# Linear attention into a snake MLP on one core: another way to turn the first chunk's q and k, and a new order table

## Chip, core and metric

The kernel runs on one core of a Trainium2 chip. The metric is the device time of one execution in microseconds (us), lower is better. Engine names: TensorE (PE) multiplies matrices and turns tiles by a matmul with the identity; VectorE (DVE) and ScalarE (ACT) do elementwise work; GpSimd (POOL) does elementwise work and issues software loads that cast fp32 to bf16 on the way; SyncE (SP) issues hardware loads and stores, which ACT can issue too. Results of TensorE lie in eight PSUM banks, everything else on chip in SBUF.

## What is computed

Inputs: q, k, v of 4 batches x 8 heads x 768 tokens x 64 features, a decay `lam` per head, and the weights of an MLP (512 to 2048 to 512 features). The reference works in blocks of 64 tokens; the kernel uses 128, which gives the same sum.

```python
Dmask = where(rel >= 0, lam ** rel, 0.0)             # rel = token i - token j, within a block
for b in range(nb):
    intra = (q_b @ k_b.T * Dmask) @ v_b
    inter = (q_b * lam ** (pos + 1)) @ kv_state
    out[block b] = intra + inter
    kv_state = lam ** block * kv_state + (k_b * lam ** (block - 1 - pos)).T @ v_b
x = out, all heads side by side                       # 3072 x 512
h = x @ w_in
g = h + sin(alpha * h) ** 2 / (alpha + 1e-09)
result = g @ w_out                                    # 3072 x 512
```

## The kernel before

There are six chunks of 128 tokens (t = 0 to 5), each with all four batches. A chunk's attention gives `xt[t]` (512 features x 512 columns of 4 batches x 128 tokens); the MLP of the same group g = t follows, in 16 slices f of 128 hidden features. Attention of later chunks is laid between the MLP work of earlier groups.

Nothing schedules by itself: every engine runs its instructions in the order in which the program issues them, and after a hand-written start that order is the table `ORDER`, one word per step. `h g.f:bank` is a hidden slice (four matmuls of 512 columns, L325), `s` its sine on ACT (L330), `q`, `Q` and `P` its square on ACT (L336), on DVE as a multiply (L338) or on DVE in a three-operand form (L340), `t` the finish on DVE that writes a slice of `gall` and frees the bank (L345). `u g.m.part` is four matmuls of the output projection with one quarter of w_out (L352), `o` its copy and store. For attention: `r`, `R`, `n`, `v` load a later chunk's k and q in the "raw" form (32 partitions, rows of four tokens) and its k and v in the natural form (token per partition), `I` and `W` load a quarter of w_in and of w_out, all through POOL. `z` scales raw q by the decay on POOL (L264), `k` and `j` turn raw k and q with DVE in pairs of bf16 values moved as fp32 (L240), `F` is the scores (L249), `m` the masks (L255), `d` scales natural k on POOL (L260), `K` makes the state's increment (L274), `S` adds it up, `B` and `C` cast it on ACT and POOL, `O` is the carried and the inner outputs (L295, L304), `x` their way into `xt`.

The mask table `C0` (L226) holds lam^-(j+1) for j not after i; the other factor lam^(i+1) is put on q ahead of the scores.

The first chunk goes another way, because there is no carried state and everything waits for it. q of batches 0 and 1 comes through SP as fp32 in rows of 64 values (L150) and is scaled by DVE (L419); q of batches 2 and 3 comes through POOL (a load of 256 KB) and is left unscaled, its factor being put on the output by the table `Etab` (L223, L416). k and v come through POOL. TensorE turns both k and q, 16 transposes each (L387), ACT or DVE copies them out of PSUM (L390, L392), `scores0` multiplies 64-row halves (L398) and masks (L403), `outs0` multiplies with v (L410) and moves the result into `xt[0]` (L414, L416). Matmuls on a constant tile (`spin`, L192) keep TensorE busy meanwhile. Then the table's words begin. The last output tile is done in two halves by `project_halves` (L367).

POOL's software loads take turns on eight semaphores, so that the ninth load waits at its issue until the first has landed.

Of the kernel before, what the change touches and what calls it, by code (L numbers as in the profile page):

```python
# [33 lines left out]
z4.0 F3.1:3054 o1.3 t2.12 u2.0.0:6 m3.1.0 h2.13:1 m3.1.1 z4.1 u2.0.1 m3.1.2 s2.13 m3.1.3 h2.14:2 j4.0 O3:7305
s2.14 Q2.13 q2.14 t2.13 t2.14 u2.0.2 x3.0 d4.0 j4.1 x3.1 h2.15:4 x3.2 x3.3 F4.0:1273 s2.15 d4.1 h3.0:0 m4.0.0
q2.15 m4.0.1 h3.1:5 s3.0 t2.15 h3.2:1 q3.0 m4.0.2 s3.1 t3.0 K4:24 s3.2 m4.0.3 u2.0.3 q3.1 S4.0 q3.2 h3.3:7 t3.1
o2.0 B4.0 u2.1.0:0 t3.2 r5 s3.3 S4.1 F4.1:3265 q3.3 u2.1.1 m4.1.0 B4.1 m4.1.1 h3.4:1 R5 m4.1.2 u2.1.2 m4.1.3
s3.4 t3.3 h3.5:4 q3.4 t3.4 v5 O4:3265 s3.5 k5.0 q3.5 u2.1.3 x4.0 t3.5 x4.1 k5.1 h3.6:7 x4.2 x4.3 h3.7:1 z5.0
o2.1 s3.6 u2.2.0:3 s3.7 h3.8:4 q3.6 z5.1 j5.0 q3.7 u2.2.1 s3.8 t3.6 F5.0:2650 q3.8 t3.7 u2.2.2 t3.8 h3.9:7
m5.0.0 m5.0.1 u2.2.3 s3.9 m5.0.2 h3.10:1 q3.9 m5.0.3 o2.2 u2.3.0:4 t3.9 s3.10 j5.1 h3.11:2 q3.10 t3.10 u2.3.1  # L40
s3.11 q3.11 F5.1:6503 u2.3.2 t3.11 m5.1.0 h3.12:7 m5.1.1 u2.3.3 m5.1.2 s3.12 m5.1.3 h3.13:1 q3.12 o2.3 t3.12
O5:2650 s3.13 q3.13 t3.13 u3.0.0:3 h3.14:4 u3.0.1 s3.14 h3.15:7 q3.14 t3.14 u3.0.2 x5.0 x5.1 h4.0:1 x5.2 x5.3
h4.1:4 s3.15 h4.2:2 s4.0 q3.15 h4.3:6 q4.0 t3.15 h4.4:5 s4.1 t4.0 s4.2 u3.0.3 q4.1 q4.2 h4.5:0 t4.1 o3.0 t4.2
u3.1.0:7 s4.3 s4.4 h4.6:1 q4.3 u3.1.1 q4.4 t4.3 s4.5 h4.7:4 t4.4 s4.6 u3.1.2 q4.5 q4.6 t4.5 h4.8:3 s4.7 t4.6
u3.1.3 q4.7 s4.8 t4.7 h4.9:2 o3.1 q4.8 u3.2.0:6 s4.9 t4.8 h4.10:5 q4.9 u3.2.1 t4.9 s4.10 u4.0.0:0 q4.10 t4.10
u3.2.2 h4.11:1 u3.2.3 s4.11 u4.0.1 q4.11 o3.2 t4.11 h4.12:4 u4.0.2 s4.12 h4.13:7 q4.12 t4.12 h4.14:3 s4.13
u4.1.0:2 q4.13 s4.14 t4.13 h4.15:5 q4.14 u4.1.1 t4.14 s4.15 h5.0:6 q4.15 t4.15 u4.1.2 s5.0 u4.0.3 q5.0 u4.1.3
o4.0 h5.1:1 o4.1 u3.3.0:4 s5.1 u4.2.0:7 q5.1 u3.3.1 h5.2:3 u3.3.2 s5.2 u4.2.1 q5.2 u3.3.3 h5.3:5 t5.0 o3.3
u4.2.2 t5.1 s5.3 t5.2 h5.4:0 q5.3 t5.3 u4.2.3 s5.4 h5.5:2 q5.4 o4.2 t5.4 u4.3.0:4 s5.5 h5.6:6 q5.5 t5.5 u4.3.1
s5.6 h5.7:1 q5.6 t5.6 u4.3.2 s5.7 h5.8:3 q5.7 t5.7 u4.3.3 s5.8 h5.9:5 q5.8 o4.3 t5.8 h5.10:7 s5.9 u5.0.0:0 q5.9  # L50
s5.10 t5.9 h5.11:2 q5.10 u5.0.1 t5.10 s5.11 h5.12:6 q5.11 t5.11 h5.13:1 s5.12 u5.0.2 q5.12 s5.13 t5.12 h5.14:4
q5.13 u5.1.0:3 t5.13 s5.14 h5.15:5 q5.14 t5.14 u5.1.1 s5.15 u5.2.0:7 q5.15 t5.15 u5.1.2 u5.0.3 u5.1.3 o5.0
u5.2.1 o5.1 u5.2.2 u5.2.3 o5.2
# [4 lines left out]
def kernel(  # L58
# [11 lines left out]
    nc = tc.nc  # L70
# [77 lines left out]
    raw_q0 = gbp.tile([P, 2, H, D], FP32, name="raw_q0", tag="gall")  # L148
    for b in range(2):
        nc.sync.dma_start(out=raw_q0[:, b], in_=q[b, :, 0:T, :].rearrange("h p e -> p h e"))  # L150
    alpha_fp = consts.tile([NFC, P], FP32, name="alpha_fp")
    A.dma_start(out=alpha_fp[:], in_=moe_alpha.rearrange("(f p) -> f p", p=P))
    new_nat(0, "k")
    new_nat(0, "v")
    nat["q", 0] = rawp.tile([P, B, H, D], BF16, name="raw_q")
    load_nat(0, "k", 0)
    load_nat(0, "k", 1)
    pcol = consts.tile([P, 3], FP32, name="pcol")

    def token_column(n, base, step):  # L160
        G.iota(out=pcol[:, n:n + 1], pattern=[[0, 1]], base=base, channel_multiplier=step,
               allow_small_or_imprecise_dtypes=True)
# [48 lines left out]
    def power(tab, n):  # L211
        A.activation(out=tab[:], in_=lnlam[:], func=ACTF.Exp, scale=pcol[:, n:n + 1])
# [312 lines left out]
```

## Time and profile before

| what | us |
|---|---|
| median of 3 runs (210.4 to 211.32) | 211.24 |
| the profiled execution | 212.47 |
| its span, first to last instruction | 210.8 |
| TensorE busy in it | 197.1 |
| ACT busy | 148.1 |
| DVE busy | 135.7 |
| POOL busy | 100.8 |

Busy times overlap. A matmul is counted from its start to the end of its result, so a mean of 0.38 us per matmul of 512 columns is its latency; they start 0.216 us apart when nothing is waited for. A line of a group reads: code line, engine, operation, what is written from what, shapes, count, busy time and mean in ns, idle time of the engine before it and what ended that. A line of the chain reads: start, length, what. "DMA w_out" there is the time from a load's issue to its landing. Landing times of single loads come from the semaphore events of the trace, of which a load has 16, one for each DMA engine. About one matmul record in thirty is missing.

### The profile page before, as it was taken

How to read it: one execution, taken by the hardware profiler on the slowest of the kernel's cores; microseconds unless marked ns; L12 is line 12 of the kernel's file. 1: busy time of each engine (PE TensorE's matmuls, PEld its weight loads, DVE VectorE, ACT ScalarE, POOL GpSimd, SP SyncE). 2: the span in 40 equal slices, each digit the busy share in tenths (PEclk: the TensorE clock that was granted, in tenths of full speed). 3: DMA queues.
4: the chain of work that ended last, by engine and by line, in shares of the span. 5: the costliest groups of instructions: out<-in, count | busy, mean ns of one | idle time of the engine just before them, and what ended most of it. 6: DMA issues, size and time to landing. Idle time of an engine off the chain costs nothing.

```text
span 210.8 us, 4860 instructions
## 1 busy us (share of the span) xinstructions
PE 197.1 (94%) x1992; PEld 97.7 (46%) x2021; DVE 135.7 (64%) x201; ACT 148.1 (70%) x258; POOL 100.8 (48%) x116
## 2 busy tenths in 40 slices
PE   7958988699999999999999999999999999999993
PEld 3543433345444455444554544544444444444452
DVE  3996789571989998699999967715551503445400
ACT  4684959005998945998697968569975855889531
POOL 7999749758999994997694600000000000000000
PEclk9999999799999999999999999999999999999999
DMA  8999999999999699499969911100111020100022
GB/s 124 156 151 182 205 193 162 165 197 166 229 165 166 77 145 183 48 142 157 157 75 166 116 53 50 51 2 0 53 50 50 0 100 35 70 16 33 0 105 98
DMA packets 68920, 22.61 MB, mean 107 GB/s; under 512 B 50834, under 2 KB 65954, under 8 KB 68898
## 3 DMA queue, kind: packets, MB, share of 16 engines
q0 software_dynamic: 63184, 15.47, 79.6%
q1 hardware_dynamic: 5680, 6.82, 9.4%
q8 instruction: 16, 0.26, 0.5%
q14 instruction: 6, 0.05, 0.1%
q10 hardware_dynamic: 34, 0.01, 0.0%
HBM read 31.47 MB, written 6.29 MB: 179 GB/s over the span
## 4 chain that ended last, share of the span: by engine, by line
PE 74%; DMA 11%; DVE 5%; POOL 4%; ACT 2%; issue 2%; DVEq 0%; ACTq 0%; POOLq 0%
PE ops L352 35%; PE hps L325 29%; DMA w_in<-in_moe_w_in_dram 4%; DMA w_out<-in_moe_w_out_dram 4%; DMA nat_k<-in_k_dram 3%; PE F_ps L249 3%; PE O_ps L304 2%; DVE gall L345 2%; POOL nat_k L260 2%; DVE STm L255 2%; PE hps L367 2%; PE O_ps L295 2%; POOL w_in L141 1%; DVE S L283 1%; PE T_ps L387 1%
## 5 line engine op out<-in xcount | busy, mean ns | idle before, releaser
L345 DVE SCALAR_TENSOR_TENSOR gall<-s,r_sb,hps 128x512 bf16<-128x512 bf16 x96 | 69.3, 742 | 46.9 <-ACT s L336 36.8
L325 PE MATMUL hps<-xt,w_in 128*128 128x512 bf16 x372 | 90.9, 379 | 2.0 <-issue 0.7
L352 PE MATMUL ops<-w_out,gall 128*128 128x512 bf16 x352 | 88.1, 382 | 4.0 <-DMA w_out<-in_moe_w_out_dram 2.4
L330 ACT ACTIVATE s_sb<-hps,alpha_sb 128x512 bf16<-128x512 f32 x96 | 64.2, 692 | 27.7 <-PE hps L325 27.5
L325 PEld LDWEIGHTS <-w_in 128*128 128x128 bf16 x384 | 36.7, 98 | 46.0 <-issue 2.2
L352 PEld LDWEIGHTS <-gall 128*128 128x128 bf16 x368 | 35.1, 98 | 44.8 <-issue 3.7
L336 ACT ACTIVATE s<-s_sb 128x512 bf16<-128x512 bf16 x86 | 52.9, 638 | 1.6
L255 DVE TENSOR_TENSOR STm<-F_ps,C 128x512 bf16<-128x512 f32 x40 | 25.0, 683 | 4.2 <-PE F_ps L249 4.1
L260 POOL TENSOR_TENSOR nat_k<-nat_k,R 128x1024 bf16<-128x1024 bf16 x10 | 19.1, 1933 | 4.5 <-DMA nat_k<-in_k_dram 4.4
L264 POOL TENSOR_TENSOR raw_q<-raw_q,Rraw 128x1024 bf16<-128x1024 bf16 x10 | 18.9, 1919 | 4.0 <-DMA raw_q<-in_q_dram 4.0
L314 ACT CAST xt<-O_ps 128x512 bf16<-128x512 f32 x20 | 10.3, 600 | 14.9 <-PE O_ps L304 14.5
L358 ACT COPY o_sb<-ops 128x512 f32<-128x512 f32 x23 | 13.5, 592 | 8.0 <-PE ops L352 6.2
L240 DVE STREAM_TRANSPOSE turned_q<-raw_q 128x512 f32<-128x512 f32 x10 | 11.1, 1114 | 5.6 <-POOL raw_q L264 5.6
L131 POOL DMA_DIRECT2D nat_v<-in_v_dram x12 | 14.0, 1170 | 0.2 <-issue 0.2
L124 POOL DMA_DIRECT2D raw_k<-in_k_dram x20 | 11.7, 598 | 3.9 <-DMA w_out<-in_moe_w_out_dram 2.9
L124 POOL DMA_DIRECT2D raw_q<-in_q_dram x20 | 11.6, 588 | 4.0 <-DMA w_in<-in_moe_w_in_dram 2.6
L131 POOL DMA_DIRECT2D nat_k<-in_k_dram x10 | 11.8, 1190 | 0.8 <-POOLq L509 0.8
L240 DVE STREAM_TRANSPOSE turned_k<-raw_k 128x512 f32<-128x512 f32 x10 | 11.0, 1117 | 0.1
L338 DVE TENSOR_TENSOR s<-s_sb 128x512 bf16<-128x512 bf16 x9 | 5.9, 657 | 2.4 <-ACT s_sb L330 2.4
L249 PEld LDWEIGHTS <-turned_k 32*128 32x128 bf16 x320 | 5.0, 96 | 4.6 <-issue 3.8
L249 PE MATMUL F_ps<-turned_q,turned_k 32*128 32x128 bf16 x320 | 6.8, 224 | 0.0
L192 PE MATMUL spare<-fill 128*128 128x512 bf16 x11 | 5.0, 607 | 1.5 <-DVE one L174 1.5
(68 smaller groups left out, 97.9 us busy)
## 6 DMA issues: line engine op xcount, KB each, us to landing
out_dram<-o_sb SPq DMA_DIRECT2D x23, 256.0 KB, 2.6
nat_v<-in_v_dram POOLq DMA_DIRECT2D x12, 256.0 KB, 7.4
nat_k<-in_k_dram POOLq DMA_DIRECT2D x10, 256.0 KB, 7.6
raw_k<-in_k_dram POOLq DMA_DIRECT2D x20, 128.0 KB, 7.3
raw_q<-in_q_dram POOLq DMA_DIRECT2D x20, 128.0 KB, 5.6
w_out<-in_moe_w_out_dram POOLq DMA_DIRECT2D x4, 512.0 KB, 9.6
w_in<-in_moe_w_in_dram POOLq DMA_DIRECT2D x6, 256.0 KB, 8.1
raw_q<-in_q_dram SPq DMA_DIRECT2D x2, 256.0 KB, 3.6
```

The costliest lines, as they stand in the source:

```text
L124: (eng or G).dma_start(out=dst[quad[a], bs].rearrange("t b n r d -> t (b n) (r d)"), in_=src[t, a])
L131: G.dma_start(out=nat[nm, t][:, bs].rearrange("p b h e -> p (b h) e"), in_=SRC[nm][bs, :, t * T:(t + 1) * T, :].rearrange("b h p e -> p (b ...
L240: V.transpose(out=dst.rearrange("p (x t r) -> p x r t", r=R, t=32), in_=src.rearrange("p (x r d) -> p x r d", r=R, d=32))
L249: nc.tensor.matmul(out=F[a][:, u, n, :], lhsT=KQ["k", t][quad[a], 2 * pr + u, n, :, e], rhs=KQ["q", t][quad[a], 2 * pr + u, n, :, e], star ...
L255: V.tensor_tensor(out=st[t, pr][:, a], in0=att["F", pr][a], in1=C0[:, a].unsqueeze(1).broadcast_to([P, 2, NQ, T]), op=ALU.mult)
L260: G.tensor_tensor(out=kd, in0=kd, in1=R128[:].unsqueeze(1).unsqueeze(3).broadcast_to([P, 2, H, D]), op=ALU.mult)
L264: G.tensor_tensor(out=qs, in0=qs, in1=Rraw[:].rearrange("p n r -> p (n r)").unsqueeze(1).unsqueeze(3).broadcast_to([P, 2, NQ * R, D]), op= ...
L325: nc.tensor.matmul(out=hps[g, f][:], lhsT=w_in_sb[f // 4][:, c, (f % 4) * P:(f % 4 + 1) * P], rhs=xt[g][:, c, :], start=(c == 0), stop=(c ...
L330: A.activation(out=s_of[g, f][:], in_=hps[g, f][:], func=ACTF.Sin, scale=alpha_sb[:, f:f + 1])
L336: A.activation(out=s2_of[g, f][:], in_=s_sb[:], func=ACTF.Square)
L345: V.scalar_tensor_tensor(out=gall[g][:, f, :], in0=s2_of.pop((g, f))[:], scalar=r_sb[:, f:f + 1], in1=hps.pop((g, f))[:], op0=ALU.mult, op ...
L352: nc.tensor.matmul(out=ops[g, m][:], lhsT=gall[g][:, f, m * P:(m + 1) * P], rhs=w_out_sb[part][:, f % 4, :], start=(f == 0), stop=(f == NF ...
```

## The change

In the first chunk, all of q comes as fp32 in the raw form (rows of 1 KB) in eight hardware loads, six by SP and two by ACT. DVE casts it to bf16 and turns it as in later chunks. k is loaded by POOL per batch for the first two batches, and turned by TensorE with the even and the odd features as separate tiles, so that the scores run in the form of later chunks (32-row quarters, two products added). q isn't scaled at all: a mask table `C1` of its own holds lam^(i-j), made by eight Exps on ACT and four selects on POOL. `C0` for later chunks is made after the first chunk's last output. The tables of powers for q and five of twelve spins are gone. The order table is new from end to end: 29 squares move from ACT to DVE, all of w_in is loaded ahead of w_out, in group 0 the products with w_out come after all sixteen hidden slices, and the final halves are a word of their own.

```diff
 ORDER = """
-I1 W0 d0.0 I2 h0.0:2 d0.1 h0.1:4 s0.0 h0.2:5 s0.1 Q0.0 I3 t0.0 K0:73 s0.2 Q0.1 h0.3:6 S0.0 r1 t0.1 q0.2 C0.0
-h0.4:0 s0.3 t0.2 S0.1 h0.5:1 q0.3 h0.6:2 C0.1 s0.4 t0.3 s0.5 h0.7:7 R1 q0.4 u0.0.0:4 q0.5 t0.4 s0.6 u0.1.0:5
-t0.5 s0.7 Q0.6 h0.8:3 t0.6 h0.9:6 Q0.7 s0.8 t0.7 h0.10:0 s0.9 Q0.8 t0.8 W1 h0.11:1 s0.10 Q0.9 W2 h0.12:2 t0.9
-q0.10 s0.11 v1 t0.10 h0.13:7 s0.12 k1.0 h0.14:3 q0.11 q0.12 t0.11 h0.15:6 s0.13 W3 t0.12 s0.14 u0.2.0:0 k1.1
-q0.13 z1.0 u0.3.0:1 q0.14 t0.13 s0.15 t0.14 q0.15 z1.1 j1.0 u0.0.1 t0.15 u0.1.1 j1.1 F1.0:2736 R2 u0.2.1 m1.0.0
...
+h0.0:7 h0.1:3 s0.0 P0.0 s0.1 t0.0 h0.2:1 h0.3:6 I1 h0.4:2 q0.1 t0.1 s0.2 s0.3 h0.5:3 d0.0 q0.2 Q0.3 t0.3 I2 t0.2
+s0.4 q0.4 t0.4 s0.5 h0.6:0 s0.6 h0.7:6 s0.7 h0.8:7 Q0.5 t0.5 h0.9:1 q0.6 Q0.7 d0.1 I3 R1 t0.7 s0.8 Q0.8 t0.6
+t0.8 s0.9 q0.9 h0.10:5 h0.11:2 W0 h0.12:4 s0.10 P0.10 s0.11 h0.13:6 s0.12 r1 W1 t0.9 t0.10 q0.11 t0.11 q0.12
+t0.12 h0.14:1 s0.13 s0.14 z1.0 q0.13 W2 j1.0 v1 q0.14 h0.15:3 t0.13 t0.14 K0:02 s0.15 q0.15 t0.15 k1.0 u0.1.0:7
+u0.2.0:4 u0.0.0:6 S0.1 C0.1 S0.0 u0.3.0:1 k1.1 F1.0:3250 W3 m1.0.2 m1.0.0 m1.0.3 u0.3.1 C0.0 z1.1 u0.2.1 m1.0.1
+u0.0.1 u0.2.2 j1.1 F1.1:2035 m1.1.0 m1.1.2 m1.1.1 m1.1.3 u0.1.1 u0.0.2 u0.3.2 O1:2350 x1.0 x1.2 x1.1 u0.1.2
...
-    raw_q0 = gbp.tile([P, 2, H, D], FP32, name="raw_q0", tag="gall")
-    for b in range(2):
-        nc.sync.dma_start(out=raw_q0[:, b], in_=q[b, :, 0:T, :].rearrange("h p e -> p h e"))
+    raw_q0 = gbp.tile([P, B, NQ, R, D], FP32, name="raw_q0", tag="gall")
...
+    for pr in range(2):
+        for a in range(NA):
+            load_raw(0, "q", a, pr, eng=nc.sync if a < 3 else A, dst=raw_q0)
+        if pr == 0:
+            A.dma_start(out=alpha_fp[:], in_=moe_alpha.rearrange("(f p) -> f p", p=P))
...
+    def load_nat0(b):
+        G.dma_start(out=nat["k", 0][:, b], in_=k[b, :, 0:T, :].rearrange("h p e -> p h e"))
+
+    load_nat0(0)
+    load_nat0(1)
...
-    load_nat(0, "q", 1)
+    delta = consts.tile([P, T], FP32, name="delta")
+    G.iota(out=delta[:], pattern=[[1, T]], base=0, channel_multiplier=-1, allow_small_or_imprecise_dtypes=True)
...
+    load_nat(0, "k", 1)
...
-    spin(7, 3)
...
+    a_ps = bank("a_ps", 5)
+    nc.tensor.transpose(out=a_ps[:, 0:NFC], in_=alpha_fp[:], identity=idf[:])
+    spin(4, 3)
...
-    def powers():
-        for a in range(NA):
-            A.activation(out=Etab[:, a, :], in_=pos_row[:], func=ACTF.Exp, scale=ln_a[:, a:a + 1])
+    def decays(a):
+        for n in range(NQ):
+            A.activation(out=C1[:, a, n, :], in_=delta[:], func=ACTF.Exp, scale=lnlam[:, 4 * n + a:4 * n + a + 1])
+        G.affine_select(out=C1[:, a], in_=C1[:, a], pattern=[[0, NQ], [1, T]], compare_op=ALU.is_ge, fill=0.0, base=0,
+                        channel_multiplier=-1)
...
-                        nc.tensor.matmul(out=F[a][:, u, n, :], lhsT=KQ["k", t][quad[a], 2 * pr + u, n, :, e],
+                        kt = KQ["k", t][quad[a], 2 * pr + u, n]
+                        nc.tensor.matmul(out=F[a][:, u, n, :], lhsT=kt[:, :, e] if t else kt[:, e, :],
...
+    def turn_k0(bs, n_bank, engs):
+        ps = psum.tile([P, len(bs), NQ, 2, T], BF16, name="T_ps", tag=f"b{n_bank}")
+        for u, b in enumerate(bs):
+            cols = nat["k", 0][:, b].rearrange("p h d -> p (h d)").rearrange("p (n m e) -> p n e m", n=NQ, e=2)
+            for n in range(NQ):
+                for e in range(2):
+                    nc.tensor.transpose(out=ps[:, u, n, e, :], in_=cols[:, n, e], identity=iden[:])
+        dst = KQ["k", 0][:, bs[0]:bs[0] + len(bs)]
...
+    def cast_q0(pr):
+        bs = slice(2 * pr, 2 * pr + 2)
+        V.tensor_copy(out=raw["q", 0][:, bs], in_=raw_q0[:, bs])
...
+    decays(0)
+    decays(1)
+    decays(2)
+    A.copy(out=alpha_sb[:], in_=a_ps[:, 0:NFC])
+    cast_q0(0)
+    turn(0, "q", 0)
+    cast_q0(1)
+    turn(0, "q", 1)
+    turn_k0((0,), 4, A)
+    turn_k0((1,), 7, A)
+    load_w_in(0, 2)
+    decays(3)
...
+    scores(0, 0, (0, 1, 2, 3))
+    turn_k0((2, 3), 6, A)
+    for a in range(NA):
+        mask(0, 0, a)
+    power(NE, 0)
+    power(R128, 1)
...
+    scores(0, 1, (4, 5, 6, 7))
+    inside0(0, (0, 1))
+    for a in range(NA):
+        mask(0, 1, a)
+    leave0(0, 0, A)
+    leave0(0, 1, A)
...
+    inside0(1, (2, 3))
+    leave0(1, 0, A)
+    leave0(1, 1, V)
+    V.reciprocal(out=r_sb[:], in_=alpha_sb[:])
+    mask_table()
```

`inside0` is the product of masked scores and v for a pair of batches, 16 matmuls into two banks; `leave0` copies one bank into `xt[0]`. `scores`, `mask` and `turn` are the functions of later chunks; `mask` takes `C1` where t is 0.

More of the change, by code (lines that the diff above doesn't have):

```diff
@@ L394, in scores0 @@
-    def scores0(b, bks):
-        F = [bank("F_ps", n)[:].rearrange("p (c i) -> p c i", c=NDC) for n in bks]
-        for c in range(NDC):
-            for n in range(2):
-                nc.tensor.matmul(out=F[n][:, c, :], lhsT=by_half["k"][half[n], b, c, :], rhs=by_half["q"][half[n], b, c, :],
-                                 start=True, stop=True)
-        st0[b] = work.tile([P, 2, NDC, T], BF16, name="STm")
-        by_pair = C0[:].rearrange("p (x y) n t -> p y n x t", y=2)
-        for n in range(2):
-            V.tensor_tensor(out=st0[b][:, n].rearrange("p (n x) t -> p n x t", n=NQ),
-                            in0=F[n].rearrange("p (n x) t -> p n x t", n=NQ), in1=by_pair[:, n], op=ALU.mult)
@@ L406, in outs0 @@
-    def outs0(b, bk):
-        O = bank("O_ps", bk)[:].rearrange("p (a i) -> p a i", a=NA)
-        for a in range(NA):
-            for n in range(NQ):
-                nc.tensor.matmul(out=O[half[n], a, :], lhsT=nat["v", 0][:, b, 4 * n + a, :], rhs=st0[b][:, a % 2, 2 * n + a // 2, :],
-                                 start=(a == 0), stop=True, skip_group_check=True)
-        x = xt[0][:, :, b * T:(b + 1) * T]
-        if b < 2:
-            A.copy(out=x, in_=O)
-        else:
-            V.tensor_tensor(out=x, in0=O, in1=Etab[:], op=ALU.mult)
@@ new lines, in inside0 @@
+    def inside0(pr, bks):
+        O = [bank("O_ps", n)[:].rearrange("p (a u i) -> p a u i", a=2, u=2) for n in bks]
+        for a in range(NA):
+            for u in range(2):
+                for n in range(NQ):
+                    nc.tensor.matmul(out=O[a // 2][half[n], a % 2, u, :], lhsT=nat["v", 0][:, 2 * pr + u, 4 * n + a, :],
+                                     rhs=st[0, pr][:, a, u, n, :], start=(a % 2 == 0 and u == 0), stop=True,
+                                     skip_group_check=True)
+        att["O0", pr] = O
```

191 lines of the change are left out of this document (75 added, 116 removed).

## The prediction

> **What bounds the kernel now.** I read the 40 slices first, then the chain of waits, then busy time by stretch, then the timeline of the start and the costliest groups.
>
> ```profile
> PE   7958988699999999999999999999999999999993
> PEclk9999999799999999999999999999999999999999
> DMA  8999999999999699499969911100111020100022
> ```
>
> A slice is 5.27 us. From slice 9 on (47 us) TensorE is full; before that it has holes while the DMA engines are full. The stretches give sizes (columns: PE, PEld, DVE, ACT, POOL busy; granted clock; DMA; GB/s):
>
> ```profile
> 26.50:36.10 9.60, 8.97 (x41) 3.93 (x41) 8.82 (x15) 7.49 (x14) 6.88 (x9) 1.00 1.33 181
> 36.10:38.50 2.40, 0.01 (x1) 0.01 (x1) 1.74 (x4) 0.93 (x2) 2.40 (x2) 1.00 1.03 151
> 38.50:43.20 4.70, 4.37 (x43) 2.07 (x44) 3.04 (x6) 0.00 (x0) 3.27 (x6) 0.64 2.09 171
> 43.20:47.00 3.80, 3.80 (x48) 1.75 (x46) 2.34 (x4) 0.00 (x0) 1.60 (x3) 1.00 1.36 199
> 47.00:207.50 160.50, 158.69 (x1647) 78.59 (x1669) 100.82 (x143) 121.18 (x208) 62.94 (x57) 1.00 0.73 90
> ```
>
> After 47 us nothing but less TensorE work could help: 158.69 of 160.50 us. At 36.1 it stands still for 2.4 us, and then the granted clock is 0.64. The chain names the cause:
>
> ```profile
> 20.67 8.87 DMA w_in<-in_moe_w_in_dram
> 29.53 0.28 issue
> 29.82 0.58 POOL raw_q L124
> 30.39 0.09 issue
> 30.48 7.97 DMA w_out<-in_moe_w_out_dram
> 38.45 0.04 issue
> 38.49 2.37 PE ops L352 x8
> ```
>
> The second quarter of w_out (word W1) lands at 38.45, and u0.0.1 waits for it. So the kernel is bound by loads up to 38.5 us and by TensorE after. By the steady starts of matmuls (216 ns for 512 columns; the chain's pieces of 4 take 0.86) the work left at 38.49 is 80 h x 0.8635 + 88 u x 0.8635 + the final halves 3.51 + 10 F x 0.57 + 5 O x 1.70 + 4 K x 0.62 = 165.3 us. The last matmul starts at 207.2, so 168.7 went by: 3.4 us lost, about 1.2 of it between 38.5 and 43.2 (half clock, gaps), the other 2.2 in small steps up to the end. After the last matmul come 3.6 us of copy and store, unchanged.
>
> **The start, part by part.**
>
> ```profile
> 0.81 1.05 SPq L150 DMA_DIRECT2D raw_q<-in_q_dram  x2
> 16.79 2.96 PE L325 MATMUL hps<-xt,w_in 128*128 128x512 bf16 x11 [0.61 <-DVE xt L416]
> 17.86 0.69 ACT L330 ACTIVATE s_sb<-hps,alpha_sb 128x512 bf16<-128x512 f32 x1 [2.88 <-PE hps L325]
> 18.57 1.82 DVE L338 TENSOR_TENSOR s<-s_sb 128x512 bf16<-128x512 bf16 x1 [1.93 <-ACT s_sb L330]
> ```
>
> The reader sees when the first hidden matmul and sine run: 16.79 and 17.86.
>
> *Loads.* Removed: one 256-KB software load of q. By the semaphore events the first five such loads land at 7.10, 9.01, 10.82, 12.63 and 14.58, so one is worth 1.81 us of full engines. Added: 512 KB more of q through the hardware queues, 1 MB in eight loads in place of 512 KB in two. Its price isn't in the trace: 2048 packets of 256 B ran from 1.9 to 4.4 (2.5 us per 512 KB, so 5.0 for 1 MB), while 1-KB packets of the last stores took 48 ns on one of 16 engines (1024 x 48/16 = 3.1). So 0.6 to 2.5 us more; I take 1.2, nearer the row with the same packet. Net -1.2 to +0.7, taken as -0.6. From w_in0 on the same loads follow up to W1 in both (I1, I2, I3, W0, R1, r1: only their order differs), and POOL has up to eight loads in flight, so W1 lands at 38.45 - 0.6 = **37.85**. POOL issues w_in0 at about 9.2 (before 10.5), so its queue doesn't run dry.
>
> *The q path.* Removed on TensorE: 16 transposes of q (1.9 us), its copies, two scalings by Rq on DVE (1.42), Etab on ACT (4 in 1.26). Added on DVE: two casts 128x1024 and two turns of 1.12 (row L240). A cast lies between 0.83 (two of L392's 0.417, half the width) and 1.5 (two of L419's 0.748, fp32 from SBUF); I take 0.95. The first pair of batches lands at 4.3 to 5.3 (5.23 today for as many bytes), the second at 7 to 10.4 (SP's last two loads wait for earlier landings, and k's software loads share the engines). So DVE is done near 9.6.
>
> *The k path and the mask table.* ACT: logarithm near 4.5, a table load 1.28, six of the eight new Exps at 0.32 to 7.7, alpha's copy, two copies of turned k at 0.58: 9.05. Four POOL selects of some 0.6 (twice the 0.31 of 128x128) fit before the masks. Then scores 0.57, four masks from 9.8 (0.65 each) to 12.4; k's second half (8 transposes, a copy of 1.01) is hidden behind these; four masks to 15.0, the last four inside matmuls, a leave of 0.58: first hidden matmul near **16.5**, against 16.79. The start itself gives about nothing. The C0 table (1.21 on DVE, moved behind it) is hidden by h0.0, h0.1 and the first sine; without this cover it costs 1.2.
>
> *Group 0.* Today ACT and DVE need 21.2 us, from 17.86 to the last finish at 39.1, among it 1.8 us of ACT waiting for h0.8, whose w_in lands at 27.2 behind W0. The new order has W0 behind all of w_in, and DVE has one turn rather than three before the last finish (-2.2). So 17.65 + 21.2 - 1.8 - 2.2 = 34.9; ACT alone has 16 sines at 0.69 and 10 squares at 0.63, 17.4 us, which gives 35.0; by today's pace without the turns' gain 37.0. I take **36.0**. Turn k1.0 follows (37.1), then F1.0.
>
> *The sum.* F1.0 (0.57) now runs before W1's products: the work left at 37.85 is 164.7. Behind it come 2.2 us of small steps as today, 0.5 of waiting for W2 (3.1 us after W1, with 2.6 us of products between), and 0.4 as one chance in three of the half clock's 1.2. Last matmul at 37.85 + 164.7 + 3.1 = 205.65, against 207.2: **-1.5 us**. The profiled execution took 212.47 (span 210.8 and 1.7 around it), 0.6% above the median of 211.24; I take the difference from the median: **209.7**.
>
> *Groups 1 to 5.* 29 squares go from ACT to DVE. Counted along the table with the rows' durations, from h1.0 to F5.1 TensorE has 76.0 us and DVE 76.2 today, 79.5 and 79.4 then; the smallest lead of TensorE's work over what it needs from DVE is 4.1 to 6 us in both. So I cost it at nothing; the cover is that lead. What takes it away:
>
> ```profile
> L338 DVE TENSOR_TENSOR s<-s_sb 128x512 bf16<-128x512 bf16 x9 | 5.9, 657 | 2.4 <-ACT s_sb L330 2.4
> L340 DVE SCALAR_TENSOR_TENSOR s<-s_sb 128x512 bf16<-128x512 bf16 x1 | 0.7, 684 | 0.0
> ```
>
> Seven of the nine squares take 0.42; the two that met a POOL multiply took 1.82 and 1.16. Groups 1 to 3, where POOL multiplies, get six such squares for three: at most 3 x 1.4 us of DVE, inside the lead. The Trainium skill (GPSIMD Engine Reference, Key points) says that GpSimd shares its SBUF interfaces with any DVE instruction of two SBUF inputs, which would include the other form (P, L340); no row has one beside a multiply. By that rule five more would be long, and the lead would be gone in one group; by the row they take 0.68.
>
> **The rivals.** *The turned q comes late (slower).* Place: DVE's casts and turns before the first mask. With the second pair landing at 10.4 and casts of 1.5, DVE is done at 13 rather than 9.6, and the hidden matmuls start at 19.8, group 0 ends at 39.2, F1.0 starts at 40.3: last matmul 40.3 + 165.3 + 2.6 = 208.2, which is 212.2; a first stretch at half clock (427 for 216 ns) puts 1.3 on that, 213.5. It decides from F1.0 at 39.3 on, that is a first sine after 19.9. For it: 12 spins become 7 and the clock reached full only at 9.04. Against it: ACT's chain ends as late as 9.05 by itself. Of this the Trainium skill (TensorE: Matmul & The Clock Gate, Part 1) says that some 3.4 us of sustained work release the clock and an idle window throttles it again; here 2.4 idle us were enough for 3.4 us of half clock.
>
> *The load is late all the same (no change).* W1 took 3.5 us behind the load before it, W0 2.3. If q's extra 512 KB costs its upper bound, W1 lands at 38.9 to 39.1 and TensorE waits as today: 38.45 + 0.55 + 164.7 + 3.1 = 206.8, which is 210.8.
>
> *DVE loses its lead in groups 1 to 3* through long squares: two to three of 1.2 us come through, 205.65 + 3 = 208.7: 212.7. For it: POOL's sixteen multiplies of 1.9 us fill 40% of that stretch. Against it: six squares alone can meet them, and TensorE lost next to nothing there today with DVE as full.
>
> *More than forecast.* W1 as short as W0 (-1.1) and group 0 done at 35.0: 36.7 + 164.7 + 2.7 = 204.1: 208.1.
>
> **How the numbers follow.** Forecast 0.37, late q 0.24, no change 0.20, DVE 0.09, more 0.10. About 0.5% (1.06 us) is what a measurement of this kernel can tell from no change. Faster by more than that: 0.34 of the forecast, all of "more" and a little of the others, 0.46. Within: most of "no change", the mild end of the late q, 0.26. Slower: 0.28. The forecast's own range is 208.7 to 210.6; the range with the others runs from 207.2 ("more", with the loads at their lower bound, -0.6, and without the half clock, -0.4) to 213.3, just short of the late q's upper end.
>
> **What would show it.** In the new profile: W1 landing near 37.9; the first hidden matmul near 16.5 and first sine before 18.5; the last finish of group 0 near 36; F1.0 before u0.3.1; no stretch after 47 us with TensorE under 98%. It is wrong if the first sine is later than 19.9, if W1 lands after 39, or if TensorE waits for DVE in groups 1 to 3.

## The result, and the profile after

| | before | changed |
|---|---|---|
| median of 22 executions each, us | 210.86 (209.62 to 212.59) | 213.53 (211.25 to 219.78) |
| ratio, with its 95% interval | | 1.0083 [1.0056, 1.0111] |
| the profiled execution and its span | 212.47, 210.8 | 213.61, 211.8 |
| first hidden matmul, first sine | 16.79, 17.86 | 18.32, 20.28 |
| last finish of group 0, F1.0 | 39.1, 40.78 | 38.54, 39.73 |
| start of the last matmul | 207.22 | 208.12 |

The change made the kernel slower, by 0.8%. The ratio leaves out eight long executions of the changed kernel, at 214.6 to 219.8 us (its others end at 214.4), which the median in the table holds. Seven of the eight took 217.7 us or more; the experiments on the squares deal with their cause.

The 40 slices of the changed kernel first, then its stretches (columns: PE, PEld, DVE, ACT, POOL busy; granted clock; DMA; GB/s):

```profile
PE   4677998999999998999999999999999999999993
PEclk9999999999999999999999999999999999999999
DMA  7999999989999889999029997200201010101042
```

```profile
18.30:36.10 17.80, 16.73 (x126) 7.27 (x127) 15.21 (x23) 13.91 (x24) 13.62 (x17) 1.00 1.26 189
36.10:38.50 2.40, 2.35 (x27) 1.11 (x16) 2.40 (x5) 2.37 (x5) 0.20 (x1) 1.00 1.47 194
38.50:43.20 4.70, 4.65 (x52) 2.22 (x51) 4.70 (x8) 0.22 (x1) 3.60 (x4) 1.00 1.98 174
43.20:47.00 3.80, 3.69 (x47) 1.68 (x46) 3.08 (x5) 0.00 (x0) 2.59 (x5) 1.00 0.73 100
47.00:208.40 161.40, 158.55 (x1649) 78.68 (x1668) 112.87 (x170) 106.13 (x179) 64.81 (x60) 1.00 0.72 91
```

The 2.4 us in which TensorE stood still at 36.1 are gone: 2.35 of 2.40 are busy. The holes are in the first three slices instead (4, 6, 7 where before had 7, 9, 5). The chain of waits between 34 and 43 us (start, length, what) no longer has the load of w_out; it lies on DVE:

```profile
35.65 1.05 DVE turned_q L242
36.70 1.22 DVE gall L348 x3
38.47 2.03 DVE turned_k L242 x2
40.49 2.43 DVE STm L258 x4
```

W1 landed at 36.75 and nothing waited for it; F1.0 waited for k1.0, which stands behind group 0's finishes on DVE. From F1.0 to the last matmul it is 168.4 us, 3.1 more than the 165.3 us of work left, as in the prediction. So what was lost against the forecast was lost ahead of 39.7 us. The timeline of the start (start, length, engine, line, what, and in brackets the idle time before it with what ended it):

```profile
5.60 0.26 PE L206 MATMUL a_ps<-idf,alpha_fp 16*128 16x16 f32 x1 [1.47 <-DMA alpha_fp<-in_moe_alpha_dram]
...
9.29 0.85 DVE L414 CAST raw_q<-raw_q 128x1024 bf16<-128x1024 f32 x1 [0.98 <-DMA raw_q<-in_q_dram]
9.61 0.61 PE L387 MATMUL T_ps<-iden,nat_k 128*128 128x128 bf16 x4 [1.50 <-DMA nat_k<-in_k_dram]
...
10.15 1.36 PE L252 MATMUL F_ps<-turned_q,turned_k 32*128 32x128 bf16 x32
10.17 1.09 DVE L242 STREAM_TRANSPOSE turned_q<-raw_q 128x512 f32<-128x512 f32 x1
10.25 0.58 ACT L390 COPY turned_k<-T_ps 128x512 bf16<-128x512 bf16 x1 [1.53 <-PE T_ps L387]
...
11.60 2.49 DVE L258 TENSOR_TENSOR STm<-F_ps,C 128x512 bf16<-128x512 f32 x4 [0.34 <-PE F_ps L252]
...
13.57 1.04 PE L252 MATMUL F_ps<-turned_q,turned_k 32*128 32x128 bf16 x32 [1.10 <-ACT turned_k L390]
...
18.32 0.58 PE L328 MATMUL hps<-xt,w_in 128*128 128x512 bf16 x1 [0.71 <-ACT xt L408]
...
19.13 2.34 PE L328 MATMUL hps<-xt,w_in 128*128 128x512 bf16 x5 [0.22 <-issue]
...
20.28 0.69 ACT L333 ACTIVATE s_sb<-hps,alpha_sb 128x512 bf16<-128x512 f32 x1 [2.01 <-PE hps L328]
```

Two loads are late: k's second batch (9.56) and q's second pair (9.21). The first mask starts at 11.60, where the prediction had 9.8. DVE's last turn of q ends at 11.26 and the scores that need k's second batch at 11.51, so both q and k are late, and k ends last. And TensorE works at half clock until 23.2: five hidden matmuls take 2.34 us, so 427 ns from start to start. (The row PEclk shows nothing of that, because the trace has its first clock event only there.) The squares are the other place that changed:

```profile
L341 DVE TENSOR_TENSOR s<-s_sb 128x512 bf16<-128x512 bf16 x26 | 12.3, 473 | 13.5 <-ACT s_sb L333 13.5
L343 DVE SCALAR_TENSOR_TENSOR s<-s_sb 128x512 bf16<-128x512 bf16 x13 | 10.1, 777 | 19.6 <-ACT s_sb L333 19.6
```

In this execution only three of the 39 are long (1.34, 0.83 and 1.81 us): the means are 473 and 777 ns, where undisturbed ones take 420 and about 690.

### The profile page after: what moved, and what is told of

Its sections match the earlier page's. It is cut to its first block, busy times and chain, and to the rows that moved or that the text cites. A ratio compares the mean times of both kernels' runs of the same rounds, so it can differ in the third digit from the quotient of the medians.

```text
span 211.8 us, 4901 instructions
## 1 busy us (share of the span) xinstructions
PE 197.3 (93%) x2008; PEld 97.9 (46%) x2034; DVE 149.5 (71%) x223; ACT 134.3 (63%) x233; POOL 101.6 (48%) x118
## 4 chain that ended last, share of the span: by engine, by line
PE 72%; POOL 8%; DVE 8%; DMA 6%; issue 3%; ACT 1%; DVEq 0%; ACTq 0%; POOLq 0%
PE ops L355 32%; PE hps L328 32%; DMA raw_k<-in_k_dram 4%; DMA w_in<-in_moe_w_in_dram 3%; DVE STm L258 3%; POOL w_in L141 2%; PE O_ps L307 2%; PE F_ps L252 2%; POOL nat_k L263 2%; PE ops L370 2%; DVE gall L348 2%; DVE turned_k L242 1%; PE O_ps L298 1%; PE KV_ps L277 1%; POOL nat_v L131 1%
## 5 line engine op out<-in xcount | busy, mean ns | idle before, releaser
L355 PE MATMUL ops<-w_out,gall 128*128 128x512 bf16 x354 | 86.0, 379 | 1.7 <-issue 1.1
L348 DVE SCALAR_TENSOR_TENSOR gall<-s,r_sb,hps 128x512 bf16<-128x512 bf16 x96 | 67.9, 738 | 4.7 <-ACT s L339 3.8
L328 PEld LDWEIGHTS <-w_in 128*128 128x128 bf16 x384 | 37.9, 99 | 48.5 <-issue 5.6
L339 ACT ACTIVATE s<-s_sb 128x512 bf16<-128x512 bf16 x57 | 35.0, 628 | 1.1
L258 DVE TENSOR_TENSOR STm<-F_ps,C 128x512 bf16<-128x512 f32 x48 | 30.5, 683 | 4.2 <-PE F_ps L252 4.2
L343 DVE SCALAR_TENSOR_TENSOR s<-s_sb 128x512 bf16<-128x512 bf16 x13 | 10.1, 777 | 19.6 <-ACT s_sb L333 19.6
L341 DVE TENSOR_TENSOR s<-s_sb 128x512 bf16<-128x512 bf16 x26 | 12.3, 473 | 13.5 <-ACT s_sb L333 13.5
L124 POOL DMA_DIRECT2D raw_q<-in_q_dram x20 | 11.7, 596 | 6.3 <-DVE turned_q L242 4.1
L242 DVE STREAM_TRANSPOSE turned_q<-raw_q 128x512 f32<-128x512 f32 x12 | 13.0, 1095 | 0.1
L131 POOL DMA_DIRECT2D nat_k<-in_k_dram x9 | 10.6, 1185 | 0.0
L252 PE MATMUL F_ps<-turned_q,turned_k 32*128 32x128 bf16 x384 | 8.6, 229 | 1.3 <-ACT turned_k L390 1.1
```

The source lines that it names most:

```text
L124: (eng or G).dma_start(out=dst[quad[a], bs].rearrange("t b n r d -> t (b n) (r d)"), in_=src[t, a])
L131: G.dma_start(out=nat[nm, t][:, bs].rearrange("p b h e -> p (b h) e"), in_=SRC[nm][bs, :, t * T:(t + 1) * T, :].rearrange("b h p e -> p (b ...
L242: V.transpose(out=dst.rearrange("p (x t r) -> p x r t", r=R, t=32), in_=src.rearrange("p (x r d) -> p x r d", r=R, d=32))
L252: nc.tensor.matmul(out=F[a][:, u, n, :], lhsT=kt[:, :, e] if t else kt[:, e, :], rhs=KQ["q", t][quad[a], 2 * pr + u, n, :, e], start=(e == ...
L258: V.tensor_tensor(out=st[t, pr][:, a], in0=att["F", pr][a], in1=(C0 if t else C1)[:, a].unsqueeze(1).broadcast_to([P, 2, NQ, T]), op=ALU.mult)
L328: nc.tensor.matmul(out=hps[g, f][:], lhsT=w_in_sb[f // 4][:, c, (f % 4) * P:(f % 4 + 1) * P], rhs=xt[g][:, c, :], start=(c == 0), stop=(c ...
```

## The experiments

All ratios are to the kernel before, on the same chip, with 95% intervals. "Old start" is the first chunk of the kernel before, "new start" that of the changed one.

### Which half of the change costs the time

The start and the table can be put together crosswise, since the table's words mean the same in both; the old start gets the word `e` for the final halves.

```diff
 # old_start_new_order: the kernel before
-ORDER = """I1 W0 d0.0 I2 h0.0:2 ...
+ORDER = """h0.0:7 h0.1:3 s0.0 P0.0 ...
 # new_start_old_order: the changed kernel
-ORDER = """h0.0:7 h0.1:3 s0.0 P0.0 ...
+ORDER = """I1 W0 d0.0 I2 h0.0:2 ... u5.2.3 o5.2 e5.3:01
```

> The first chunk as before, the order table (and the final halves) as after. Theory S (the whole loss sits in the new start: first hidden matmul at 18.32 instead of 16.79, first sine at 20.28 instead of 17.86): with the first sine at 17.9 group 0 ends 18.3 us later at 36.2, F1.0 runs at about 37.4, the last matmul starts near 205.8, ratio to before 0.993 (0.988 to 0.997). Theory O (the new table makes waits of its own): ratio 1.00 to 1.01, with TensorE idle in groups 1 to 3.

> The first chunk as after, the order table as before. Theory S: the start's 1.5 us and the half clock are paid here too, first sine near 20.3, group 0's last finish near 41, ratio to before 1.008 to 1.015. Theory O: the loss goes with the table, ratio 0.998 to 1.003.

Measured: 1.0041 [1.0009, 1.0074] and 1.0053 [1.0024, 1.0082]. In these two runs both halves cost something. With the old start the first sine ran at 18.87, the last finish of group 0 at 35.2, F1.0 at 36.3; with the new start and the old table the first sine ran at 20.12, and the full clock came at 21.66. So the late sine and the late clock belong to the start, whatever the table.

The same comparison later on one chip, together with the changed kernel:

> The changed kernel, unchanged, on one chip beside the next three runs. Ratio 1.005 to 1.012 among its shorter executions, and about a third of the executions 2 to 3% longer, with the square of slice 0 of group 2 held.

> As old_start_new_order (1.0041), on the same chip. If the new start costs under the new table what 1.0083 and 1.0041 say: 0.4% below after. If it costs what 1.013 and 1.0011 say (both with the squares on ACT): about 1% below after. Long executions as often as in after.

Measured: 1.0132 [1.0088, 1.0177] for the changed kernel, 1.0070 [1.0038, 1.0102] with the old start. Under the new table the start cost 0.6%, and the table 0.7%; the two intervals overlap, so the first figure is rough.

### Is it the clock?

alpha's load lands at 5.46, behind q on ACT's queue, and the spins stand behind alpha's transpose. The edit puts spins ahead of it.

```diff
+    spin(7, 3)
     a_ps = bank("a_ps", 5)
     nc.tensor.transpose(out=a_ps[:, 0:NFC], in_=alpha_fp[:], identity=idf[:])
-    spin(4, 3)
```

> After, with seven spins ahead of alpha's transpose in place of four behind it; nothing waits for alpha before TensorE is warm. If the half clock up to 23.2 us is a part of the loss (theory S): full clock by 10 us, the first sine about 1 us earlier (19.3), ratio to before 1.003 to 1.005 where after has 1.0083. If the clock costs nothing because DVE and ACT set the pace of group 0 anyway: the first sine earlier, the end as after, ratio 1.007 to 1.010.

Measured: 1.0309 [1.0257, 1.0361]. The clock was full from 7.2 to 10.6 us, and then half again to 20.85: from 7.2 to 10.6 TensorE had been busy for only 1.47 of 3.40 us. The first sine ran at 20.03, only 0.25 earlier. So it was no test of the clock, but it showed something else. All four executions took 216.2 to 218.1 us, and its timeline says why:

```profile
84.38 4.42 DVE L341 TENSOR_TENSOR s<-s_sb 128x512 bf16<-128x512 bf16 x1
84.70 3.81 POOL L263 TENSOR_TENSOR nat_k<-nat_k,R 128x1024 bf16<-128x1024 bf16 x2
...
88.83 2.72 DVE L348 SCALAR_TENSOR_TENSOR gall<-s,r_sb,hps 128x512 bf16<-128x512 bf16 x4
...
89.63 1.86 PE L355 MATMUL ops<-w_out,gall 128*128 128x512 bf16 x4 [3.36 <-DVE gall L348]
```

One square, the word Q2.0, is held for 4.42 us in place of 0.42, until 0.3 us after two POOL multiplies (d3.0, d3.1) that run back to back have ended. The finish behind it is late, TensorE waits 3.36 us for it, and then works at half clock from 89.1 to 92.5.

A second try at the start took half of q off the hardware queues as well:

```diff
-    for pr in range(2):
-        for a in range(NA):
-            load_raw(0, "q", a, pr, eng=nc.sync if a < 3 else A, dst=raw_q0)
+    for a in range(NA):
+        load_raw(0, "q", a, 0, eng=nc.sync if a < 3 else A, dst=raw_q0)
...
+    for a in range(NA):
+        load_raw(0, "q", a, 1)
...
-    cast_q0(1)
```

> As the run before, and q's second pair of batches comes through POOL as bf16 (four loads behind k's first two), without fp32 rows and without DVE's second cast. If the fp32 rows on the hardware queues are what holds up k's second batch (landed 9.56) and q's second pair (9.21): k's second batch lands before 8.5, DVE's first mask starts near 10.3 instead of 11.6, first hidden matmul near 17, ratio to before 0.996 to 1.000. If the loads only change places in a full queue: k's third and fourth batch and the mask are as late as in after, ratio as in the run before.

Measured: a median of 218.86, with no ratio (one execution took 214.0 us, three 218.8 to 219.2). k's second batch landed at 7.12 (9.56 in the changed kernel), but its third and fourth only at 11.7, and the first mask waited 1.28 us for a select on POOL, which stood behind four more load issues: 10.94. First sine 20.72. The same square was held for 4.79 us. It is inconclusive for the start: what q's loads gave was lost on POOL's queue.

To keep the clock full, spins are needed in each hole. With the squares of groups 1 to 3 on ACT (see "Are the squares on DVE held?"):

```diff
+    spin(7, 3)
     a_ps = bank("a_ps", 5)
...
-    spin(4, 3)
...
     turn_k0((0,), 4, A)
+    spin(7, 3)
     turn_k0((1,), 7, A)
...
     turn_k0((2, 3), 6, A)
+    spin(5, 5)
...
+    spin(6, 2)
     inside0(1, (2, 3))
```

> The run after_squares_on_act (ratio 1.013) with more matmuls on the constant tile: seven ahead of alpha's transpose, seven between k's first two transposes, five and six in the two later holes of the start. If the half clock up to 22 us is a part of the loss: full clock before 12 us and through group 0, first sine near 18.9 instead of 19.9, group 0's last finish near 36.3 instead of 37.8, ratio 1.003 to 1.007. If group 0 is paced by ACT and DVE whatever the clock: first sine near 18.9, last finish within 0.5 us of 37.8 less 1, ratio 1.008 to 1.011. If the added matmuls delay the real ones: first hidden matmul after 18.3.

Measured: 1.0100 [1.0063, 1.0137], against 1.0130 [1.0096, 1.0164] without the spins on another chip. The clock was full from 6.8 us on, the first sine ran at 18.58, group 0 ended at 36.1. Stretches of the changed kernel and of this one:

```profile
18.30:23.20 4.90, 4.66 (x11) 1.72 (x12) 3.55 (x5) 1.93 (x3) 4.90 (x8) 1.00 1.19 188
```

```profile
18.30:23.20 4.90, 3.75 (x18) 1.66 (x17) 4.84 (x5) 4.44 (x8) 4.90 (x5) 1.00 0.96 144
36.10:38.50 2.40, 1.34 (x35) 0.62 (x34) 1.58 (x3) 0.20 (x1) 2.40 (x4) 1.00 1.24 206
```

Between 18.3 and 23.2 it ran 18 matmuls in place of 11. But at 36.1 TensorE has its hole again (1.34 of 2.40 busy): it waits for k1.0, whose own load lands at 36.9, and for W1, which landed at 38.98 here. So the clock cost some 1.3 us of the first sine (19.93 without the spins), and most of that didn't reach the end; the intervals of the two ratios overlap.

### Is it q's loads?

The four hardware loads of q's second pair are left out and the second cast reads the first pair, so the outputs of batches 2 and 3 of the first chunk use the q of batches 0 and 1; every other instruction stays. Squares of groups 1 to 3 on ACT.

```diff
-        for a in range(NA):
+        for a in range(NA if pr == 0 else 0):
             load_raw(0, "q", a, pr, eng=nc.sync if a < 3 else A, dst=raw_q0)
...
-        V.tensor_copy(out=raw["q", 0][:, bs], in_=raw_q0[:, bs])
+        V.tensor_copy(out=raw["q", 0][:, bs], in_=raw_q0[:, 0:2])
```

> The run after_squares_on_act without the four hardware loads of q's second pair of batches (its place is taken by the first pair again, so the outputs of batches 2 and 3 in the first chunk are those of another q). This is the price of 512 KB of fp32 rows by itself. If they hold up the start: k's second batch lands near 7.6 instead of 9.2 to 9.6, the first mask starts near 10.0 instead of 11.4, the first hidden matmul near 16.7 instead of 18.0, ratio 1.006 to 1.009. If the start is held by its own chain on ACT and TensorE: first mask and first hidden matmul move by less than 0.5 us, ratio 1.011 to 1.014.

Measured: 1.0045 [1.0015, 1.0075], 0.85% below 1.0130 (on another chip), and 0.55% below the kernel with spins on the same chip. Its start:

```profile
7.20 1.06 PE L387 MATMUL T_ps<-iden,nat_k 128*128 128x128 bf16 x8
7.28 1.43 DVE L414 CAST raw_q<-raw_q 128x1024 bf16<-128x1024 f32 x1
...
9.71 1.88 DVE L258 TENSOR_TENSOR STm<-F_ps,C 128x512 bf16<-128x512 f32 x3
...
16.82 0.58 PE L328 MATMUL hps<-xt,w_in 128*128 128x512 bf16 x1 [0.70 <-ACT xt L408]
...
18.79 0.69 ACT L333 ACTIVATE s_sb<-hps,alpha_sb 128x512 bf16<-128x512 f32 x1 [2.01 <-PE hps L328]
```

Without these 512 KB, k's second batch lands at 6.59 rather than 9.56, its eight transposes run in one go, the first mask starts at 9.71 (9.8 in the prediction) and the first hidden matmul at 16.82 (16.5). A later mask still waited 0.98 us for a select on POOL, and the clock was still half from 13.1 to 19.9. So the start's late masks are the price of q's second half: without it neither q nor k is late.

### Are the squares on DVE held?

```diff
 # after_q2_0_on_act: one word
-... m3.0.0 Q2.0 t2.0 s2.1 q2.1
+... m3.0.0 q2.0 t2.0 s2.1 q2.1
 # after_squares_on_act: all 11 of groups 1 to 3
-... s1.1 P1.0 q1.1 ... Q2.0 ... Q2.6 ... P2.9 ... P2.13 ... Q3.2 ... P3.4 ...
+... s1.1 q1.0 q1.1 ... q2.0 ... q2.6 ... q2.9 ... q2.13 ... q3.2 ... q3.4 ...
```

> After, with one square changed: that of slice 0 in group 2 (word Q2.0) goes to ACT. In the run named warm DVE spent 4.42 us on it, between two POOL multiplies (84.70 to 88.50), TensorE waited 3.4 us for the finish and then ran 3.4 us at half clock. Theory H (a DVE instruction with two SBUF inputs is held for as long as POOL multiplies): no such wait at 80 to 95 us, no half clock there, no execution above 215, ratio to before 1.004 to 1.008. Rival (the wait comes from somewhere else, as a load): the finish of the slice is as late, executions at 217 remain.

> After, with all 13 DVE squares of groups 1 to 3 on ACT, as nearly all of these are in before. Theory H with the start as the rest of the loss: the waits of TensorE for DVE between 78 and 110 us go (some 1 us), ratio 1.001 to 1.005, which is the start's share. If DVE's load as such is no matter and only Q2.0 is: as the run before. If ACT becomes the bound: ratio over 1.008 with waits for ACT.

> As after_squares_on_act, now beside after on the same chip. If the held squares make the long executions alone: none above 215, and the ratio equals that of after's shorter executions within 0.3%. If they also cost in the shorter ones: 0.3% or more below it. If the load on ACT costs: above it.

Measured: 1.0116 [1.0075, 1.0157], 1.0130 [1.0096, 1.0164] and 1.0143 [1.0094, 1.0192]. (The expectations speak of 13 squares; the edit moves eleven.) The 16 executions with all eleven squares on ACT lie between 211.5 and 214.9 us: those at 216 and above, 8 of the changed kernel's 28, are gone (with Q2.0 alone moved, four executions at 212.6 to 214.3, too few to tell). But the others got no faster by it. No such long execution of the changed kernel itself was profiled; the two profiles of that length, both with spins ahead of alpha's transpose, have the held Q2.0.

A short hold of the same word, in the kernel with the old start and the new table, shows how little it takes to stop TensorE:

```profile
82.31 2.33 POOL L131 DMA_DIRECT2D nat_k<-in_k_dram  x2
83.05 1.72 DVE L338 TENSOR_TENSOR s<-s_sb 128x512 bf16<-128x512 bf16 x1
...
84.61 3.81 POOL L260 TENSOR_TENSOR nat_k<-nat_k,R 128x1024 bf16<-128x1024 bf16 x2
...
85.61 1.02 PE L352 MATMUL ops<-w_out,gall 128*128 128x512 bf16 x4 [0.66 <-DVE gall L345]
```

Here the square took 1.30 us more than its 0.42, and TensorE waited 0.66: without the hold the finish would have been 0.64 us ahead of TensorE. The two long holds give the same lead, 4.00 less the wait of 3.36 and 4.37 less one of 3.73. These rows also leave something open. This hold began 1.56 us ahead of the first multiply, while POOL was issuing loads of k, so a multiply alone doesn't explain it; yet in two other profiles Q2.0 took 0.39 and 0.40 us beside such an issue. The three-operand form is held as well, here in the changed kernel on the later chip:

```profile
103.21 1.90 POOL L267 TENSOR_TENSOR raw_q<-raw_q,Rraw 128x1024 bf16<-128x1024 bf16 x1
103.21 2.45 DVE L343 SCALAR_TENSOR_TENSOR s<-s_sb 128x512 bf16<-128x512 bf16 x1 [0.68 <-ACT s_sb L333]
```

2.45 us for 0.69. The rule weighed in the prediction (the Trainium skill, GPSIMD Engine Reference, Key points: GpSimd shares its SBUF interfaces with any DVE instruction of two SBUF inputs) agrees with this row; the undisturbed 0.684 us of L340 in the first profile had no multiply beside it.

With the old start:

> The first chunk as before, the new table with the 13 squares on ACT. If start and held squares are together the whole loss: ratio 0.994 to 0.999, with no half clock behind 20 us. If the new table has other costs: ratio 1.000 to 1.004.

> As old_start_squares_on_act (1.0011): 0.998 to 1.003, no execution above 214, and 0.8 to 1.2% below after_squares_on_act_2, which is the start's price under this table.

Measured: 1.0011 [0.9975, 1.0047] and 1.0017 [0.9983, 1.0050], against 1.0041 and 1.0070 with the squares on DVE. Of the 22 executions with the squares on DVE five took 216.2 to 218.0 us; with them on ACT the longest of 22 took 213.1. So without the held squares the new table neither gains nor loses, as far as these intervals tell; and with them on ACT the new start costs 1.2% (1.0130 less 1.0011) and 1.3% (1.0143 less 1.0017), each pair on one chip. The intervals are too wide to say whether that differs from the 0.6% with the squares on DVE.

### Was the profile of before a usual one?

> The kernel before, unchanged, for a second profile: its executions lie at 209.6 to 212.6 and the first profile was of one at 212.47. If that one's stop of 2.4 us at 36.1 and its half clock at 39.8 to 43.2 are not typical: another execution near 210.6 without the half clock, last matmul start near 205.6. If they are typical: the same stop and clock, and the time comes from elsewhere.

Measured: 211.63 us, last matmul at 206.38. Its stretch, and its wait for W1:

```profile
36.10:38.50 2.40, 1.28 (x7) 0.56 (x6) 2.30 (x4) 1.06 (x2) 2.40 (x2) 1.00 1.25 158
38.50:43.20 4.70, 4.54 (x80) 2.25 (x80) 3.69 (x6) 0.00 (x0) 3.27 (x7) 1.00 2.04 175
```

```profile
37.34 1.89 PE L352 MATMUL ops<-w_out,gall 128*128 128x512 bf16 x8 [1.12 <-DMA w_out<-in_moe_w_out_dram]
```

W1 landed at 37.30 rather than 38.45, TensorE waited 1.12 us rather than some 2.4, and the clock stayed full from 38.5 to 43.2, where it had been 0.64. (It was half from 15.7 to 19.1 instead, so the first sine ran at 19.03, and yet the last matmul came 0.84 us earlier.) In the kernel with the old start and the old table that has spins and squares on ACT (last part) W1 landed at 36.94, and TensorE waited 1.49 us. So the execution that the prediction was built on had the longest stop of three; what is usual, three profiles can't settle.

### Is there a version that beats both?

Old start with spins in its two holes, and the squares that can meet a multiply on ACT; once with the old table (four squares), once with the new one.

```diff
     # in the old start, at two places
+    spin(4, 6)
...
+    spin(4, 2)
```

> Before, with its four DVE squares of groups 1 and 2 on ACT and two times four matmuls on the constant tile in the holes of the start. In two profiles of before one square was held for 1.2 to 1.6 us by a POOL multiply (TensorE waited 1.0 us at 70) and the clock fell to half for 3.4 us once. If both cost: ratio 0.991 to 0.996 and no half clock between 9 and 50 us. If the start's load of w_out hides it: 0.998 to 1.001.

> The run old_start_squares_on_act (1.0011) with the same eight matmuls in the holes of the start. If its half clock at 14.8 to 18.3 costs: first sine near 17.6 instead of 18.5, ratio 0.995 to 0.999. If the landing of W1 (37.5) sets the end in any case: 1.000 to 1.002.

> old_start_squares_on_act_warm once more, on the same chip as old_start_warm_loads. Theory: 0.996 to 1.000 again, w_out's load at 37.3 to 37.9. Rival, that the 0.9981 of the first time was the chip's: 1.001 to 1.004.

Measured: 1.0021 [0.9992, 1.0050] with the old table, 0.9981 [0.9959, 1.0004] and 0.9989 [0.9959, 1.0019] with the new one. The last two are the lowest of all, and their intervals still hold 1. The waits of the first of these two that are left:

```profile
32.56 3.61 PE L352 MATMUL ops<-w_out,gall 128*128 128x512 bf16 x15 [0.46 <-DMA w_out<-in_moe_w_out_dram]
36.57 0.64 PE L249 MATMUL F_ps<-turned_q,turned_k 32*128 32x128 bf16 x32 [0.39 <-DVE turned_k L240]
37.78 3.61 PE L352 MATMUL ops<-w_out,gall 128*128 128x512 bf16 x15 [0.57 <-DMA w_out<-in_moe_w_out_dram]
```

With the first sine at 18.19 and group 0 done at 35.0, TensorE waits for loads, W0 and then W1 (37.73). So these were put in another order, W0 and W1 ahead of R1 and r1, and the words that need the loads of R1 and r1 a little later:

```diff
-... d0.1 I3 R1 t0.7 ... h0.11:2 W0 h0.12:4 ... s0.12 r1 W1 t0.9 ... W2 j1.0 v1 q0.14 ... t0.15 k1.0 ... S0.0 u0.3.0:1 k1.1 F1.0:3250 ...
+... d0.1 I3 W0 t0.7 ... h0.11:2 W1 h0.12:4 ... s0.12 R1 r1 t0.9 ... W2 v1 q0.14 ... t0.15 j1.0 k1.0 ... S0.0 u0.3.0:1 u0.3.1 u0.2.1 u0.0.1 k1.1 F1.0:3250 ...
```

> As old_start_squares_on_act_warm (before's first chunk, the new table, the squares of groups 1 to 3 on ACT, spins in the holes of the start), with the loads behind the first chunk in another order: w_out in second place, r's first 8 pairs behind its two halves, and the scores that need r early moved behind it. Theory that there the loads up to w_out at 37 to 38 us set when TensorE fills: w_out lands by 36.2, no wait on its load over 0.5 us is left, the last matmul starts at 204.0 to 204.6 and the ratio is 0.990 to 0.996. Rival, that the wait only moves to the next load (first feature load or v1, which now land later): a wait of 1 us or more on another load between 35 and 46 us, ratio 0.997 to 1.002.

Measured: 1.0191 [1.0152, 1.0229]. W0 and W1 landed at 29.2 and 31.8, and everything behind them later:

```profile
39.43 0.64 PE L249 MATMUL F_ps<-turned_q,turned_k 32*128 32x128 bf16 x32 [1.49 <-DVE turned_k L240]
...
42.44 1.02 PE L352 MATMUL ops<-w_out,gall 128*128 128x512 bf16 x4 [1.40 <-DMA w_out<-in_moe_w_out_dram]
...
44.59 1.04 PE L249 MATMUL F_ps<-turned_q,turned_k 32*128 32x128 bf16 x32 [1.13 <-DVE turned_q L240]
```

The rival held, and worse than it had priced: three waits of 1.1 to 1.5 us, then half clock from 44.2 to 47.6, and the last matmul at 209.0. F1.0 ran at 39.43 rather than 36.57: here the loads that moved up pushed others back.

## Why the prediction was wrong

**The start** is the step that failed first: "So DVE is done near 9.6", and the masks from 9.8. The work was sized nearly right: DVE's casts (1.28 and 0.85) and turns (1.12 and 1.09) took 4.3 us, forecast 4.1. The landings were not. Being done at 9.6 with a cast and a turn still to do means q's second pair at 7.5, near the lower end of the bounds of 7 to 10.4. It landed at 9.21, and the last turn ended at 11.26. For k's second batch the text has no term at all; it landed at 9.56, and ACT's second copy of k ended at 10.83, not 9.05. The price of 512 KB more was taken as 0.6 to 2.5 us, and on the landing of W1 alone. On k's second batch it was 3.0 us (9.56 with q's second half, 6.59 without it). On W1 no run shows it: W1 landed at 36.75 here, even earlier than 37.85, but at 37.0 to 39.0 in six other profiles with the new start and the new table, and at 38.60 without q's second half. The first hidden matmul ran at 18.32 for 16.5, of which half of q's loads gives back 1.5 (16.82). The first sine at 20.28 is later than 19.9, one of the prediction's own signs of being wrong.

**The clock.** Nothing was charged to the forecast for the spins taken away, and only the rival of the late q has a first stretch at half clock. With the new start, all of q on the hardware queues and no added spins, it lasted until 21.4 to 23.5 us in six profiles. In the first of them it cost 0.8 of the 2.6 us by which the first sine came late (first hidden matmul to first sine 1.96 us, against 1.15 forecast) and more in the slices behind it.

**Group 0** came out at its size: from the first sine to the last finish 18.26 us, forecast 18.35. That is luck in part, since a half clock lay in it: with the old start the same table took 16.3 to 17.0 us. So F1.0 came at 39.73, above the 39.3 from which the rival of the late q decides. The mechanism of that rival was the right one, and its chance of 0.24 was too low; "ACT's chain ends as late as 9.05 by itself" was no argument against it, since the last two copies of that chain wait for k's loads. Its numbers fit less well than they seem to. It has the hidden matmuls at 19.8, measured 18.32, and the last matmul at 208.2 without the half clock and 209.5 with it, measured 208.12. Its 213.5 meets a median that holds the eight long executions; the other 14 have a median of 212.7.

**The baseline.** "I take the difference from the median" failed too. The profiled execution stood 1.2 us above that median and had a longer stop than two other profiles with the old table, and a half clock behind it that they lack; the forecast removed just these. The forecast's last matmul at 205.65 with the same 5.25 us behind it (212.47 less 207.22) is 210.9, the median of before. So even with the start as forecast there was nothing to gain. The runs with the old start and the new table bear this out: last matmul at 204.1 to 206.6, ratios of 0.998 to 1.007.

**The squares.** "So I cost it at nothing" rests on a lead of 4.1 to 6 us, and on long squares of 1.4 us more at most. Both were wrong in groups 1 to 3: at Q2.0 the lead was 0.64 us, and in the kernels with spins ahead of alpha's transpose a held square took 4.0 and 4.4 us more, so that TensorE waited 3.36 and 3.73 us. On the old start the table costs 0.4 and 0.7% with these squares on DVE and 0.1 and 0.2% without. **The C0 table** behind the first output took 2.0 us rather than 1.21, and no wait in the timeline goes to it.

## What to carry to other kernels

A load that is added beside others is to be priced at the landing of every load that runs with it, the smallest-packet one first, and not only at the one that bounds the kernel later. Before a forecast removes a stall, ask whether it is there in the median or only in the profiled execution; where one profile stands above the median, forecast the absolute end and not the difference. A lead is to be taken at the place where the work is moved, and not over a whole stretch. Here squares on DVE did harm beside long POOL multiplies, and a gain at the start is worth only what the next loads leave of it.

## What was not expected of the hardware

- A DVE square (two SBUF inputs) that overlaps POOL multiplies can be held until all that run back to back have ended: 0.42 us became 4.42 and 4.79. In the three-operand form 0.69 became 2.45, and there the square ended while a further multiply ran on. Others that met a multiply took their usual time, 0.42 at 28.64 in the changed kernel, and one hold began ahead of the multiply. What decides is open.
- Beside fp32 rows of 1 KB on the hardware queues (198 and 192 packets per us from 5 to 6 and from 6 to 7 us), the software loads of k moved 237 and 348 packets of 128 B per us; from 8.5 us on, with those queues empty, 1200. The Trainium skill (DMA: Bandwidth & Descriptors, Queues, rings and completion order) says that a DMA engine takes turns between its queues by packet, which it counts as several descriptors. The like numbers of packets from 5 to 6 us agree with taking turns, by which a queue of long packets gets the larger share; how much one turn holds no run here shows.
- A clock that was full at 7.2 us was taken back at 10.6, after 3.4 us of which TensorE was busy for 1.47, and stayed half until 20.85; the later half-clock stretches (39.8 to 43.2 in the first profile of before, 89.1 to 92.5 and 44.2 to 47.6 above) last 3.4 us each. Spins ahead of the holes alone gained 0.25 us on the first sine here; spins in each hole up to the first dense work gained some 1.3.
